# First loads of an MLP kernel on one queue, and the first transposes in two groups

## The chip, the cores and the metric

The kernel runs on one core of a Trainium2 chip. The metric is the device time of one execution in microseconds; 0.2% of it is about 0.8 us. A core has a matrix engine (TensorE, PE in the profile, with weight loads listed as PEld), VectorE (DVE), ScalarE (ACT), GpSimd (POOL) and SyncE (SP), which here only starts transfers. Each engine works through its own list of instructions in order, and engines wait for each other through semaphores. Transfers from memory are started by SP or ACT and carried out by 16 DMA engines.

## The reference

A layer norm without scale, a matrix product with bias, GELU, and a second product with bias. x is 2048 x 1024, w1 is 1024 x 3584, w2 is 3584 x 1024, all bf16.

```python
def _layernorm(x, axis=-1, eps=1e-5):
    m = jnp.mean(x, axis=axis, keepdims=True)
    v = jnp.var(x, axis=axis, keepdims=True)
    return (x - m) / jnp.sqrt(v + eps)

def reference(x, w1, b1, w2, b2):
    y = _layernorm(x, axis=-1)
    h = _gelu(jnp.einsum("bsd,df->bsf", y, w1) + b1)
    return jnp.einsum("bsf,fd->bsd", h, w2) + b2
```

## The kernel before

The 2048 rows of x are cut into 16 tiles of 128 and four blocks of four tiles. For each block the first product runs over 28 rows of output (`r`, 128 features each), each with 8 steps over the model dimension (`dt`, 128 each) and 512 columns (the rows of x in that block); GELU on ACT writes `hT_sb`. Then the second product makes eight output pieces of 128 x 512, each of 28 matmuls, and VectorE adds b2. Both products need their inputs with the contracted dimension on the partitions, so tiles of x are transposed.

Blocks 1 to 3 are normalised and transposed on VectorE under the matmuls of the block before. Block 0 has nothing to hide under, and its start is written out by hand; this is the part that the change touches.

**Raw tiles.** Tiles 0 to 2 (`N_RAW`) are transposed by PE before they are normalised. `pe_T` (L366) takes parts (tile, half) and a bank: the transposes of a half (four of 128 columns, `HALVES`) go to PSUM, ACT copies them to `yT_sb` (L386) and signals `te<tile>_<half>`. Matmuls run on the raw data, and the normalisation is put right afterwards: a column with a one beside the data (L259) gives each row's sum of weights, ACT copies it (`act_cs`, L526), and VectorE corrects each of the first seven PSUM banks with it and with rows that hold minus the mean and the reciprocal deviation (`ops_corr`, L535, the instructions of L537 and L540). GELU (L419) follows. `ops_fix` (L332) makes the centred `yT_sb` for the later rows of block 0.

**The first wave.** Seven rows (`R`) are held open in seven PSUM banks: rows 0 to 4 in `ps_1`, row 5 in the second bank of `ps_2`, row 6 in the first. The eighth bank, `t`, takes transposes, and the two of `ps_2` also serve for that before their rows start. `cells(rows, dts, t0, t1)` (L512) issues one matmul for each row and dt over the columns of tiles t0 to t1. It waits for the copies of those tiles and for the part of w1. Row 7 follows in bank t (`mm1_row`, L432), and row 8 reuses the bank of row 0, after row 0's GELU.

**Clock fillers.** `warm` (L484) issues matmuls on a constant, whose result is overwritten. 24 run at the start.

**Loads.** Each load is one transfer. `x0a` is the first half of tile 0's columns (128 KB); `xrb` the second halves of tiles 0 to 2 in one (384 KB); `w0` to `w7` are w1 for the first seven rows, one dt each (224 KB); `w8` and on are w1's later columns. SP issues `SP_FIRST_LOADS`, and then all others; ACT issues `x1a` and `x2a` (L227 to L230) ahead of its table load. SP spends about 0.47 us from one issue to the next.

**Order on the engines around the change.** PE: fillers, transposes of tile 0 and of tile 1 (first halves), cells of rows 0 to 4 with dt 0 and tile 0, transposes of tile 2, cells with tile 1, then both tiles together, then tile 2, then dt 2; then the second halves, which need `xrb`, and the rest of the wave; tile 3 last. VectorE (`head`, L492 to L507): statistics of the three first halves, of the three second halves, of tile 3, mean and deviation, transposes of these into rows, b1, the three fixes, the seven corrections. GpSimd spreads the rows over the partitions (L497).

Of the kernel before, what the change touches and what calls it, by code (L numbers as in the profile page):

```python
# [13 lines left out]
TPB = TB // P  # L14
R_WAVE = 7
NB1 = 5
NB2 = 2
NOB = 2
TAIL_PIECES = (384, 128)
WARM = 24  # L20
N_RAW = 3
RC = N_RAW * P
HALVES = (0, 4, 8)
W1_CHUNK_COLS = (512, 512, 1024, 640)
N_W2_CHUNKS = 4
SP_FIRST_LOADS = ("x0a", "w0", "w1", "w2", "xrb", "w3", "w4", "x3a", "x3b", "w5", "w6", "w7", "b1", "w8")
ACT_FIRST_LOADS = ("x1a", "x2a")

T_PE_START = 4.2
T_DVE_START = 26.0  # L30
# [54 lines left out]
def bass_standalone__mixer_channel_mlp__prompt_kernel(  # L85
# [13 lines left out]
    DT = D // P  # L99
# [6 lines left out]
    assert HC <= 512 and DT * P * 2 <= 2048 and FT >= 4 and FT <= P  # L106
    R = max(1, min(R_WAVE, FT - 2, NB1 + NB2))
    assert NB1 + NB2 + 1 <= 8 and NB2 == 2
    assert HALVES[-1] == DT and 0 < N_RAW < TPB

    w1_chunks = [(j, j + 1, 0, R * P) for j in range(DT)]
    c0 = R * P
# [24 lines left out]
    with ExitStack() as es:  # L137
# [32 lines left out]
        sp = _Prog(None)  # L170
        pe = _Prog("s_pe")
        act = _Prog("s_act")
# [3 lines left out]
        est = {}  # L176

        dma_bytes = [0.0]
        dma_q = [sp]
        x_ev = {}  # L180
        w1_issued = set()

        def dma(dst, src, sig, nbytes, waits=()):
            dma_q[0].op(lambda e, dst=dst, src=src: e.dma_start(dst, src), waits=waits, sig=sig, sem="d_" + sig, inc=16)
            dma_bytes[0] += nbytes
            est[sig] = DMA_T0 + dma_bytes[0] / DMA_BYTES_PER_US

        def load_x_tile(i):
            dma(x_sb[:, i, :], xf[i * P:(i + 1) * P, :], f"x{i}", P * D * 2)
            x_ev[i] = (f"x{i}", f"x{i}")  # L190
# [7 lines left out]
        def load_w1(ci):  # L198
            j0, j1, a, b = w1_chunks[ci]
            dma(w1_sb[:, j0:j1, a:b], w1v[:, j0:j1, a:b], f"w1c{ci}", (j1 - j0) * P * (b - a) * 2)  # L200
            w1_issued.add(ci)
# [5 lines left out]
        def issue(item):  # L207
            if item == "xrb":
                dma(x_sb[:, 0:N_RAW, HC:D], xf[0:N_RAW * P, HC:D].rearrange("(t p) d -> p t d", p=P), item,
                    N_RAW * P * HC * 2)  # L210
                for i in range(N_RAW):
                    x_ev[i] = (f"x{i}_0", item)
            elif item[0] == "x" and item[-1] in "ab":
                i, h = int(item[1:-1]), "ab".index(item[-1])
                dma(x_sb[:, i, h * HC:(h + 1) * HC], xf[i * P:(i + 1) * P, h * HC:(h + 1) * HC], f"x{i}_{h}",
                    P * HC * 2)
                x_ev[i] = (f"x{i}_0", f"x{i}_1")
            elif item == "b1":
                b1v = b1.rearrange("(t q a) -> q t a", q=4, a=32)
                for q in range(4):  # L220
                    dma(b1r_sb[32 * q:32 * q + FT, :], b1v[q], f"b1{q}", F // 2, waits=["b1z"])
            elif item[0] == "x":
                load_x_tile(int(item[1:]))
            elif item[0] == "w" and int(item[1:]) < len(w1_chunks):
                load_w1(int(item[1:]))

        dma_q[0] = act  # L227
        for item in ACT_FIRST_LOADS:
            issue(item)
        dma_q[0] = sp  # L230
        for item in SP_FIRST_LOADS:
            issue(item)
        for i in range(TPB):
# [16 lines left out]
        for b in range(2, NB):  # L250
# [5 lines left out]
                waits=["ones"], sig="ident")  # L256
# [11 lines left out]
        def op_stats(i, h):  # L268
            return (lambda e, i=i, h=h: e.bn_stats(st_sb[:, i, 6 * h:6 * (h + 1)], x_sb[:, i, h * HC:(h + 1) * HC]),  # L269
                    [x_ev[i][h]], f"st{i}_{h}", 0.65)  # L270

        def op_aggr(i):
            if i >= TPB:
                pool.op(lambda e, i=i: e.tensor_tensor(out=rstd_sb[:, i:i + 1], in0=mv_sb[:, i, 1:2],  # L274
                                                       in1=nhalf[:, i:i + 1], op=ALU.pow),
                        waits=[f"mv{i}", "nhalf"], sig=f"rstd{i}")
            return (lambda e, i=i: e.bn_aggr(mv_sb[:, i, :], st_sb[:, i, :]),  # L277
                    [f"st{i}_0", f"st{i}_1", "eps"], f"mv{i}", 0.33)
# [20 lines left out]
        y_ev = {}  # L299
# [32 lines left out]
        def ops_fix(i):  # L332
            s0, s1 = i * P, (i + 1) * P
            return [(lambda e: e.tensor_tensor(out=yT_sb[:, 0, :, s0:s1], in0=yT_sb[:, 1, :, s0:s1],  # L334
                                               in1=row_sb[:, 0:1, s0:s1].to_broadcast([P, DT, P]), op=ALU.add),
                     ["row0", f"te{i}_0", f"te{i}_1"], f"fx{i}v", 1.25)]

        yT_ev = {}
        mm1_done = {}
# [19 lines left out]
        def dve_put(o):  # L359
            dve.op(o[0], waits=o[1], sig=o[2])  # L360
# [4 lines left out]

        def pe_T(parts, bname):  # L366
            bap = t_bank[bname]
            nb = HALVES[1]
            last = f"tp{parts[-1][0]}_{parts[-1][1]}"
            w0 = ["ident"] + ([bank_read[bname]] if bname in bank_read else [])  # L370
            copies = []
            for n, (i, k) in enumerate(parts):
                j0, j1 = HALVES[k], HALVES[k + 1]
                buf, s0 = (1 if i < N_RAW else 0), i * P
                o = n * nb * P
                for j in range(j0, j1):
                    waits = (w0 if n == 0 else []) + [x_ev[i][k] if i < N_RAW else y_ev[i][j]] if j == j0 else []
                    pe.op(lambda e, i=i, j=j, o=o + (j - j0) * P: e.transpose(  # L378
                        out=bap[:, o:o + P], in_=x_sb[:, i, j * P:(j + 1) * P], identity=ident[:, :]),
                        waits=waits, sig=(f"tp{i}_{k}" if j == j1 - 1 else None))  # L380
                    yT_ev.setdefault(i, [None] * DT)[j] = f"te{i}_{k}"
                src = bap[:, o:o + (j1 - j0) * P].rearrange("p (j s) -> p j s", j=j1 - j0)
                copies.append((yT_sb[:, buf, j0:j1, s0:s0 + P], src, f"te{i}_{k}"))
                pe_t[0] += (j1 - j0) * 0.056
            for dst, src, sig in copies:
                act.op(lambda e, dst=dst, src=src: e.copy(out=dst, in_=src), waits=[last], sig=sig)  # L386
                bank_read[bname] = sig
# [96 lines left out]
        def warm(n, gate=None):  # L484
            for _ in range(n):
                pe.op(lambda e: e.matmul(ps_1[:, 0, 0:P], lhsT=unit, rhs=unit,  # L486
                                         start=True, stop=True), waits=[gate] if gate else [])

        act.op(lambda e: e.preload_act_table(ACT.Sqrt))
        warm(WARM)  # L490
        raw = list(range(N_RAW))
        head = [op_stats(i, h) for h in range(2) for i in raw] + [op_aggr(i) for i in raw]  # L492
# [3 lines left out]
        for k in range(2):  # L496
            pool.op(lambda e, k=k: e.partition_broadcast(  # L497
                row_sb[:, k, 0:RC], rvt_sb[0:1, k * N_RAW:(k + 1) * N_RAW, :].rearrange("p v s -> p (v s)")),
                waits=["rvt", "row1c", "scr"], sig=f"row{k}")
        pool.op(lambda e: e.tensor_tensor(out=scr_sb[:, 1, :], in0=scr_sb[:, 0, :], in1=nhalf[:, :], op=ALU.pow),  # L500
                waits=["row1"])
        h = DT // 2
        FX = [f"fx{i}v" for i in raw]
        for i in raw:
            head += ops_fix(i)
        for o in head:
            dve_put(o)  # L507

# [3 lines left out]
        def cells(rows, dts, t0, t1, by_row=False):  # L512
            n0, n1 = t0 * P, t1 * P + (1 if t1 == N_RAW else 0)
            order = [(r, dt) for r in rows for dt in dts] if by_row else [(r, dt) for dt in dts for r in rows]
            for r, dt in order:
                bank = wave[r][0]
                w = [yT_ev[i][dt] for i in range(t0, t1)] + (["rone"] if n1 > RC else [])
                if r not in started:
                    w += [bank_read[k] for k in (f"{bank[0]}_{bank[1]}",) if k in bank_read]
                pe_cell(r, dt, 1, n0, n1, bank, w, f"cw_{r}" if dt == DT - 1 and n1 > RC else None,  # L520
                        r not in started, False, shared=True)
                started.add(r)
# [26 lines left out]
        def late_cells(t, rows, dts):  # L549
            for r in rows:  # L550
# [6 lines left out]
                        act_gelu(r, 0, TPB, wave[r][0], f"sb_{r}", f"g_0_{r}")  # L557
                        hT_row[(0, r)] = f"g_0_{r}"

        first, most, every = range(NB1), [*range(NB1), R - 1], range(R)  # L560
        pe_T([(0, 0)], "t")
        pe_T([(1, 0)], "2_0")
        cells(first, (0,), 0, 1)
        pe_T([(2, 0)], "2_1")
        cells(first, (0,), 1, 2)
        cells((R - 1,), (0,), 0, 2)
        cells(most, (1,), 0, 2)
        cells((NB1,), (0, 1), 0, 2)
        cells(every, (0, 1), 2, 3)
        cells(every[:4], (2,), 0, 3)  # L570
        pe_T([(0, 1), (1, 1)], "t")
        cells(every[4:], (2,), 0, 3)
        cells(first, (3,), 0, 3)
        pe_T([(2, 1)], "t")
        cells(every[NB1:], (3,), 0, 3)
        act.op(lambda e: e.activation(out=std_sb[:, :], in_=mv_sb[:, 0:TPB, 1], func=ACT.Sqrt, bias=0.0, scale=1.0),
               waits=[f"mv{i}" for i in range(TPB)], sig="std")
# [52 lines left out]
        while ci < len(crit) or fi < len(fill):  # L630
# [5 lines left out]
            if take_crit:  # L636
                rdy, o, _ = crit[ci]
                ci += 1
            else:
                rdy, o, _ = fill[fi]  # L640
# [46 lines left out]
```

## Time and profile before

| What | us |
|---|---|
| Runs shown: median (lowest to highest of three) | 396.92 (396.49 to 397.13) |
| The profiled execution: its time, its span | 397.14, 395.9 |
| PE busy in the span | 393.0 |
| First filler on PE | 0.83 |
| First transposes of tile 0, start | 3.50 |
| First copy by ACT, start and length | 4.12, 0.585 |
| First cell, start | 4.76 |
| Second halves (`xrb`): issue on SP, statistics of them on VectorE | 2.64, 8.18 |
| Their transposes on PE, start | 8.63 |
| Last first-layer matmul of row 7, row 8's first | 20.71, 20.87 |

The landings of the first loads, from the trace (the last of 16 DMA engines): x0a 3.36, x1a 3.54, w0 4.60, x2a 4.77, w1 5.97, w2 6.54, `xrb` 8.16, w3 8.88, w4 9.48, x3a 9.82, x3b 10.19, w5 10.79, w6 11.39, w7 12.01, w8 16.49.

A line of a group gives the engine, the line of the kernel, the operation, its output and input tiles and shapes, and the count; in a timeline the first two numbers are the start and the length in us, and in brackets stands how long the engine was idle before and which event ended that. The chain of waits gives start, length, engine, tile, line and count. A matmul's recorded length includes its passage through the array, so successive ones overlap, and the distance of their starts tells the rate.

### The profile page before, as it was taken

The numbers are of one execution on the slowest core, as the hardware profiler recorded it, in microseconds if no ns is written. First come the engines' busy times: TensorE is split into PE (matmuls) and PEld (weight loads), VectorE is DVE, ScalarE is ACT, GpSimd is POOL, SyncE is SP. The second block draws the span as 40 slices with busy tenths as digits, with TensorE's granted clock in tenths as the row PEclk, the third lists the DMA queues.
The fourth block names the chain that finished last, engine by engine and source line by source line (L and its number), as shares of the span: only waits on it lengthen the run. The fifth ranks groups of instructions, "written<-read, shape, count | busy, mean of one in ns | idle before, by whom it ended". The sixth has DMA issues, their size and how long they took to land.

```text
span 395.9 us, 4579 instructions
## 1 busy us (share of the span) xinstructions
PE 393.0 (99%) x1964; PEld 186.6 (47%) x1964; DVE 160.1 (40%) x336; ACT 83.7 (21%) x125; POOL 11.9 (3%) x28
## 2 busy tenths in 40 slices
PE   8999999999999999999999999999999999999998
PEld 7744444444444444444444444444444444444445
DVE  4998889988999405987100000001100000001011
ACT  3374330000144342000023443100003334400000
POOL 0121100011000100000000000000000000000000
DMA  7999940000000000000000000000000000000000
GB/s 256 365 378 387 388 167 14 28 26 14 28 0 0 2 0 2 27 17 24 26 13 2 0 0 2 13 13 28 21 21 13 0 2 0 0 15 26 13 28 27
DMA packets 16747, 23.62 MB, mean 60 GB/s; under 512 B 1240, under 2 KB 10456, under 8 KB 16728
## 3 DMA queue, kind: packets, MB, share of 16 engines
q1 hardware_dynamic: 16440, 23.08, 16.6%
q8 instruction: 15, 0.25, 0.3%
q10 hardware_dynamic: 288, 0.26, 0.2%
q14 instruction: 4, 0.03, 0.0%
HBM read 19.14 MB, written 4.19 MB: 59 GB/s over the span
## 4 chain that ended last, share of the span: by engine, by line
PE 99%; ACT 0%; DVE 0%; issue 0%
PE ps L462 49%; PE ps L410 41%; PE ps_t L410 8%; PE ps L486 1%; PE ps_t L378 0%; ACT yT_sb L386 0%; PE ps L378 0%; DVE o_sb L473 0%
## 5 line engine op out<-in xcount | busy, mean ns | idle before, releaser
L462 PE MATMUL ps<-w_sb,hT_sb 128*128 128x512 bf16 (+2 forms) x924 | 194.1, 373 | 0.0
L410 PE MATMUL ps<-yT_sb,w_sb 128*128 128x512 bf16 (+4 forms) x832 | 167.1, 360 | 0.3 <-ACT yT_sb L386 0.3
L462 PEld LDWEIGHTS ps<-w_sb,hT_sb 128*128 128x128 bf16 x924 | 89.3, 98 | 104.5
L410 PEld LDWEIGHTS ps<-yT_sb,w_sb 128*128 128x128 bf16 x832 | 78.1, 98 | 84.8 <-ACT yT_sb L386 0.5
L419 ACT ACTIVATE hT_sb<-ps,b_sb 128x512 bf16<-128x512 f32 x94 | 64.2, 688 | 235.6 <-PE ps L410 217.2
L473 DVE TENSOR_TENSOR o_sb<-ps,b_sb 128x512 bf16<-128x512 f32 (+2 forms) x33 | 22.3, 676 | 198.5 <-PE ps L462 198.4
L354 DVE STREAM_TRANSPOSE yT_sb<-x_sb 32x256 bf16<-32x256 bf16 x192 | 83.7, 436 | 21.6 <-PE ps_t L410 18.6
L410 PE MATMUL ps_t<-yT_sb,w_sb 128*128 128x512 bf16 (+2 forms) x152 | 34.0, 368 | 0.0
L269 DVE BATCH_NORM_STATS2 st_sb<-x_sb 128x6 f32<-128x512 bf16 x32 | 21.1, 674 | 6.0 <-DMA x_sb<-in_x_dram 5.8
L410 PEld LDWEIGHTS ps_t<-yT_sb,w_sb 128*128 128x128 bf16 x152 | 14.5, 98 | 16.4
L419 ACT ACTIVATE hT_sb<-ps_t,b_sb 128x512 bf16<-128x512 f32 x18 | 12.4, 687 | 18.0 <-PE ps_t L410 14.6
L545 DVE TENSOR_TENSOR ps<-ps,row_sb 128x384 f32<-128x384 f32 x17 | 9.3, 564 | 3.1 <-PE ps L410 2.7
L274 POOL TENSOR_TENSOR rstd_sb<-mv_sb,nhalf 128x1 f32<-128x1 f32 x12 | 6.5, 542 | 99.6 <-DVE mv_sb L277 99.6
L294 DVE TENSOR_SCALAR x_sb<-x_sb,mv_sb,rstd_sb 128x1024 bf16<-128x1024 bf16 x13 | 7.0, 541 | 1.9 <-POOL rstd_sb L274 1.3
L386 ACT COPY yT_sb<-ps_t 128x512 bf16<-128x512 bf16 x6 | 3.3, 587 | 4.9 <-PE ps_t L378 4.9
L537 DVE SCALAR_TENSOR_TENSOR ps<-row_sb,cs_sb,ps 128x385 f32<-128x385 f32 x7 | 4.3, 615 | 0.0
L540 DVE TENSOR_TENSOR ps<-ps,row_sb 128x385 f32<-128x385 f32 x7 | 4.0, 568 | 0.2
L277 DVE BATCH_NORM_AGGREGATE mv_sb<-st_sb 128x2 f32<-128x15 f32 x16 | 3.3, 214 | 1.2
L334 DVE TENSOR_TENSOR yT_sb<-yT_sb,row_sb 128x1024 bf16<-128x1024 bf16 x3 | 3.7, 1293 | 0.0
L486 PE MATMUL ps<-const-bfloat16-1.0 128*128 128x128 bf16 x24 | 2.7, 312 | 0.8 <-PEq L672 0.8
L500 POOL TENSOR_TENSOR scr_sb<-scr_sb,nhalf 128x16 f32<-128x16 f32 x1 | 2.9, 2947 | 8.4 <-issue 8.4
L486 PEld LDWEIGHTS ps<-const-bfloat16-1.0 128*128 128x128 bf16 x24 | 2.5, 148 | 0.8 <-issue 0.8
(33 smaller groups left out, 18.7 us busy)
## 6 DMA issues: line engine op xcount, KB each, us to landing
w_sb<-in_w_dram SPq DMA_DIRECT2D x4, 1792.0 KB, 18.1
out_dram<-o_sb SPq DMA_DIRECT2D x31, 128.0 KB, 1.7
x_sb<-in_x_dram SPq DMA_DIRECT2D x3, 1024.0 KB, 14.0
w_sb<-in_w_dram SPq DMA_DIRECT2D x2, 1024.0 KB, 9.2
w_sb<-in_w_dram SPq DMA_DIRECT2D x1, 2048.0 KB, 15.2
w_sb<-in_w_dram SPq DMA_DIRECT2D x8, 224.0 KB, 5.7
w_sb<-in_w_dram SPq DMA_DIRECT2D x1, 1280.0 KB, 16.3
x_sb<-in_x_dram SPq DMA_DIRECT2D x3, 128.0 KB, 5.6
```

Of the source, the lines that this page charges most:

```text
L269: return (lambda e, i=i, h=h: e.bn_stats(st_sb[:, i, 6 * h:6 * (h + 1)], x_sb[:, i, h * HC:(h + 1) * HC]), [x_ev[i][h]], f"st{i}_{h}", 0.65)
L274: pool.op(lambda e, i=i: e.tensor_tensor(out=rstd_sb[:, i:i + 1], in0=mv_sb[:, i, 1:2], in1=nhalf[:, i:i + 1], op=ALU.pow), waits=[f"mv{i} ...
L294: return (lambda e, i=i, c0=c0, c1=c1: e.tensor_scalar(out=x_sb[:, i, c0:c1], in0=x_sb[:, i, c0:c1], scalar1=mv_sb[:, i, 0:1], scalar2=rst ...
L354: res.append((lambda e, src=src, dst=dst: e.transpose(out=dst, in_=src), waits, (f"tr{i}" if lastop else None), 0.47))
L410: pe.op(lambda e: e.matmul(unit_bank(bank)[:, n0:n1], lhsT=w1_sb[:, dt, r * P:(r + 1) * P], rhs=yT_sb[:, buf, dt, n0:n1], start=start, sto ...
L419: act.op(lambda e, r=r, n0=n0, n1=n1, bank=bank: e.activation(out=hT_sb[:, r, n0:n1], in_=unit_bank(bank)[:, n0:n1], func=ACT.Gelu_apprx_tanh,
L462: pe.op(lambda e, st=st, ft=ft, c0=c0, c1=c1, bank=bank: e.matmul(ps_2[:, bank, 0:c1 - c0], lhsT=hT_sb[:, ft, st * P:(st + 1) * P], rhs=w2 ...
L473: crit.append((est[sig], (lambda e, ob=ob, c0=c0, c1=c1, bank=bank: e.tensor_tensor(out=o_sb[:, ob, c0:c1], in0=ps_2[:, bank, 0:c1 - c0], ...
L486: pe.op(lambda e: e.matmul(ps_1[:, 0, 0:P], lhsT=unit, rhs=unit, start=True, stop=True), waits=[gate] if gate else [])
L537: return [(lambda e: e.scalar_tensor_tensor(out=ap, in0=row_sb[:, 0, :], scalar=cs_ap[r], in1=ap, op0=ALU.mult, op1=ALU.add), [f"m1_0_{r}" ...
L540: (lambda e: e.tensor_tensor(out=ap, in0=ap, in1=row_sb[:, 1, :], op=ALU.mult), [f"sa_{r}", "row1"], f"sb_{r}", 0.56)]
L545: crit.append((est[wait_ev], (lambda e: e.tensor_tensor(out=ap, in0=ap, in1=row_sb[:, 1, 0:RC], op=ALU.mult), [wait_ev, "row1"], f"sc_{r}" ...
```

## The change

- ACT issues no loads any more. SP issues all, in the order x0a, w0, x1a, w1, x2a, w2, `xrb`, and on as before.
- The first half of tile 0 is transposed in two groups of two 128-column pieces, into two banks, with a copy of 256 columns each (`PARTS` in place of `HALVES`). Cells wait for the group that holds their dt.
- Three of the 24 fillers move behind these transposes.
- The cells that follow are reordered: dt 0 and dt 1 of tile 0 on their own, and then both of tile 1 on their own, where before dt 1 took both tiles at once. Tile 2's transposes come before tile 1's cells, in bank t.
- The three fixes are put into VectorE's list at a later place of the text; nothing else is put there between.

```diff
-WARM = 24
+WARM = 21
+FILL = 3
-HALVES = (0, 4, 8)
+PARTS = ((0, 4), (4, 8), (0, 2), (2, 4))
-SP_FIRST_LOADS = ("x0a", "w0", "w1", "w2", "xrb", "w3", "w4", "x3a", "x3b", "w5", "w6", "w7", "b1", "w8")
-ACT_FIRST_LOADS = ("x1a", "x2a")
+SP_FIRST_LOADS = ("x0a", "w0", "x1a", "w1", "x2a", "w2", "xrb", "w3", "w4", "x3a", "x3b", "w5", "w6", "w7", "b1", "w8")
...
-        dma_q[0] = act
-        for item in ACT_FIRST_LOADS:
-            issue(item)
-        dma_q[0] = sp
         for item in SP_FIRST_LOADS:
             issue(item)
...
-                     ["row0", f"te{i}_0", f"te{i}_1"], f"fx{i}v", 1.25)]
+                     ["row0"] + list(dict.fromkeys(yT_ev[i])), f"fx{i}v", 1.25)]
...
-            nb = HALVES[1]
+            nb = DT // 2
-                j0, j1 = HALVES[k], HALVES[k + 1]
+                j0, j1 = PARTS[k]
-                    waits = (w0 if n == 0 else []) + [x_ev[i][k] if i < N_RAW else y_ev[i][j]] if j == j0 else []
+                    waits = (w0 if n == 0 else []) + [x_ev[i][j // nb] if i < N_RAW else y_ev[i][j]] if j == j0 else []
...
-        first, most, every = range(NB1), [*range(NB1), R - 1], range(R)
-        pe_T([(0, 0)], "t")
-        pe_T([(1, 0)], "2_0")
+        first, every = range(NB1), range(R)
+        pe_T([(0, 2)], "t")
+        pe_T([(0, 3)], "2_0")
+        warm(FILL)
         cells(first, (0,), 0, 1)
-        pe_T([(2, 0)], "2_1")
-        cells(first, (0,), 1, 2)
-        cells((R - 1,), (0,), 0, 2)
-        cells(most, (1,), 0, 2)
-        cells((NB1,), (0, 1), 0, 2)
+        pe_T([(1, 0)], "2_1")
+        cells(first, (1,), 0, 1)
+        pe_T([(2, 0)], "t")
+        cells(first, (0, 1), 1, 2)
+        cells((R - 1, NB1), (0, 1), 0, 2, True)
         cells(every, (0, 1), 2, 3)
```

More of the change, by code (lines that the diff above doesn't have):

```diff
@@ L108, in bass_standalone__mixer_channel_mlp__prompt_kernel @@
     assert NB1 + NB2 + 1 <= 8 and NB2 == 2
-    assert HALVES[-1] == DT and 0 < N_RAW < TPB
+    assert PARTS[1][1] == DT and 0 < N_RAW < TPB
     w1_chunks = [(j, j + 1, 0, R * P) for j in range(DT)]
@@ L178, in bass_standalone__mixer_channel_mlp__prompt_kernel @@
         dma_bytes = [0.0]
-        dma_q = [sp]
         x_ev = {}
@@ L183, in dma @@
         def dma(dst, src, sig, nbytes, waits=()):
-            dma_q[0].op(lambda e, dst=dst, src=src: e.dma_start(dst, src), waits=waits, sig=sig, sem="d_" + sig, inc=16)
+            sp.op(lambda e, dst=dst, src=src: e.dma_start(dst, src), waits=waits, sig=sig, sem="d_" + sig, inc=16)
             dma_bytes[0] += nbytes
@@ L503, in bass_standalone__mixer_channel_mlp__prompt_kernel @@
         FX = [f"fx{i}v" for i in raw]
-        for i in raw:
-            head += ops_fix(i)
         for o in head:
@@ L574, in bass_standalone__mixer_channel_mlp__prompt_kernel @@
         pe_T([(2, 1)], "t")
+        for i in raw:
+            for o in ops_fix(i):
+                dve_put(o)
         cells(every[NB1:], (3,), 0, 3)
```

## The prediction

> **What bounds the kernel now.** I read the page first (busy time, then the chain that ended last), then the chain in order of time for the first 22 us, then the timeline of each engine there, the waits, and the issues and landings of the first loads. On the page TensorE is the bound:
>
> ```profile
> span 395.9 us, 4579 instructions
> ...
> PE 393.0 (99%) x1964; PEld 186.6 (47%) x1964; DVE 160.1 (40%) x336; ACT 83.7 (21%) x125; POOL 11.9 (3%) x28
> ...
> PE 99%; ACT 0%; DVE 0%; issue 0%
> ```
>
> From 20.87 us to 394 us PE never pauses, so this change can move only the time at which PE reaches that dense part. The chain up to there (start, duration, what):
>
> ```profile
> 0.83 2.72 PE ps L486 x24
> 3.54 0.55 PE ps_t L378 x4
> 4.10 0.02 issue
> 4.12 0.59 ACT yT_sb L386
> 4.72 0.05 issue
> 4.76 0.72 PE ps L410 x5
> 5.48 0.43 PE ps L378 x4
> 5.91 2.89 PE ps L410 x32
> 8.79 0.45 PE ps_t L378 x8
> ```
>
> The reader is to see three things. The 24 fillers end just before the first transposes. PE then idles while ACT copies tile 0 (the only real gap). And the clock is low at first: four transposes take 0.43 us at 5.48, eight take 0.45 us at 8.79. In the timeline, 128-column matmuls start 107 ns apart until 6.12 us and 56 ns apart afterwards; I call 6.12 the switch.
>
> At the other end of the ramp stands a second bound, which the chain doesn't show because it ends in a tie. The timeline around 20.8 us:
>
> ```profile
> 20.22 0.81 PE L410 MATMUL ps_t<-yT_sb,w_sb 128*128 128x384 bf16 x4
> 20.83 0.14 PEld L410 LDWEIGHTS ps<-yT_sb,w_sb 128*128 128x128 bf16 x2 [0.18 <-ACT hT_sb L419]
> 20.87 0.38 PE L410 MATMUL ps<-yT_sb,w_sb 128*128 128x512 bf16 x1
> ```
>
> Row 8 of block 0 reuses the PSUM bank of row 0, so its weight load waits for row 0's GELU (20.09 to 20.78). PE's own arrival is 20.71 + 0.16 = 20.87: no time is lost, and none is spare. What feeds that GELU is VectorE, almost without a gap since one load:
>
> ```profile
> 3.39 2.10 DVE L269 BATCH_NORM_STATS2 st_sb<-x_sb 128x6 f32<-128x512 bf16 x3 [2.19 <-DMA x_sb<-in_x_dram]
> 8.18 1.88 DVE L269 BATCH_NORM_STATS2 st_sb<-x_sb 128x6 f32<-128x512 bf16 x3 [2.69 <-DMA x_sb<-in_x_dram]
> ...
> 15.19 3.73 DVE L334 TENSOR_TENSOR yT_sb<-yT_sb,row_sb 128x1024 bf16<-128x1024 bf16 x3
> 18.85 0.61 DVE L537 SCALAR_TENSOR_TENSOR ps<-row_sb,cs_sb,ps 128x385 f32<-128x385 f32 x1
> ```
>
> The second line waits for `xrb`, the second halves of tiles 0 to 2, issued at 2.64 and landing 5.5 us later:
>
> ```profile
> x_sb<-in_x_dram SPq DMA_DIRECT2D x1, 384.0 KB, 5.5
> ```
>
> So the dense part begins at the later of two times: PE's own arrival, and `xrb`'s landing (8.16) + 12.6 us of VectorE and ACT work + 0.1. Both are 20.87 today.
>
> **The change, part by part.**
>
> *x0a alone at the head.* Today x0a and x1a share the DMA engines and land at 3.36 and 3.54; the transposes start at 3.50. The stretch from 2 to 3 us moved 287 GB/s, that from 3.4 to 5.0 moved 359. No row shows x0a alone. Bounds: nothing saved, or all of x1a's 131 KB taken out from ahead of its end, 131/355 = 0.37 us. Since the two interleaved nearly packet for packet I take 0.37: transposes at T = 3.13.
>
> *Three fillers fewer at the start.* 3 x 107 ns = 0.32; the last leaves its slot at 3.02 instead of 3.34. PE waits for x0a there anyway, so this is worth nothing; if x0a is not earlier, PE idles 0.48 instead of 0.16.
>
> *Tile 0 in two groups.* Before: four transposes, copy of 512 columns, first cell 1.26 after T (3.50 to 4.76). After: two transposes end at T + 0.37, ACT starts 0.04 later, copies 256 columns. ACT copies took 0.585 for 512 columns and 0.165 for 5, so 256 cost 0.375; 0.055 to PE: first cell at T + 0.84 = 3.97. That is 0.42 less. The extra copy costs ACT about 0.16 us of fixed time; ACT was idle from 5.20 to 5.94 and from 6.53 to 9.28, which hides it.
>
> *Three fillers behind the transposes*: T + 0.43 to T + 0.75, before the copy is done at T + 0.78, so hidden; with the clock up they take 0.17, hidden still.
>
> *Cells reordered.* Five 256-column cells become ten of 128: 2 x 57 - 109 = 5 ns each, 0.02 us in all.
>
> *Banks.* Tile 2 now goes through bank t, whose copy of tile 0 is long read; the `xrb` transposes then wait for tile 2's copy, done by about 6.8, against 8.5. Row 5 and 6's cells wait for copies done by 6. Nothing.
>
> *The fixes' place in the text.* VectorE's order is the same; the first fix waits for three copies instead of two, all over by 10.4, against 15.19. Nothing.
>
> *Two issues off ACT's queue* (0.89 us): the table load can start at 0.8 instead of 1.70 and end at 2.1. First copy after 3.5, so nothing.
>
> *Two issues more on SP.* SP spends 0.47 us per issue, so everything behind x2a is issued up to 0.95 later: w2 (0.95), `xrb` (2.64 to 3.58), w3, w4, x3a, x3b, w5 to w7, the four parts of b1, w8. No load waits for another's data; what counts is whether the issue becomes later than the turn of its data. x0a's first packet came 1.02 after its issue; `xrb`'s came at 5.08, which is 2.44 after. So 1.42 is spare against 0.95, and the bytes ahead of `xrb` are the same 1.08 MB. Its landing stays at 8.16; the bounds are -0.4 (fifteen of its engines had landed by 8.03, ten by 7.44) and +0.95. w8 turns tight (issue about 9.55 + 1.02 = 10.57, its data's turn 10.27), 0.3 late at most, and it landed at 16.49 for a use at 19.1. x3a and x3b have 0.4 and 0.6 us on VectorE, w5 to w7 more than 1 us on PE, b1 1.7.
>
> The Trainium skill, "DMA: Bandwidth & Descriptors", section "Issuing engines are not separate DMA queues", says that transfers started by several engines share the same 16 DMA engines and that issuing from several saves only the sequencer's issue time. That speaks against this change: it would give 0.95 us of issue time back to SP for nothing in bandwidth. If that time stood on the path the sum would be 397.9; by the 1.42 us of spare lead it is hidden, and the forecast stands.
>
> *The other landings.* By the bytes ahead, interpolated between today's landings (0.32 MB at 3.54, 0.62 MB at 4.77, 0.85 MB at 5.20 on fifteen engines and 5.97 on the last): w0 at 3.7 (today 4.60), x1a 4.2, w1 5.0, x2a 5.2 to 6.0 (today 4.77), w2 as today.
>
> *PE's new order in time, low clock to 6.12.* Cells of tile 0, dt 0, 3.97 to 4.51; tile 1's transposes to 4.93; dt 1 waits for w1, 5.0 to 5.55; tile 2's transposes to 5.97; then ten cells of tile 1, two at 107 and eight at 57, to 6.6; 4 x 109, 14 x 57, 4 x 163 to 8.49. Today the `xrb` transposes start at 8.63: a lead of about 0.14, or a lag of 0.15 where x2a lands at 6.0. The 0.8 us won at the first cell has shrunk because 0.32 of it is fillers, the rest ran at half the clock, and the switch stays where it is.
>
> **Sum.** Lead at 8.5: 0.14. At 20.87 the GELU of row 0 hasn't moved, so what is kept is what the weight load had spare, 0.04 at most. The profiled run of 397.14 (span 395.9 and 1.24 around it) would become 397.10. The shown runs have a median of 396.92, 0.22 less; to that I apply the same 0.04 and round: **396.9**, no change that can be told. Own range, from the bounds of `xrb` short of a late issue and of x2a: 396.5 to 397.4.
>
> **Rivals.**
>
> *The later issue reaches `xrb`.* Slower. Place: SP's queue; it decides once the lead of issue over first packet falls under 0.95. Price: VectorE's whole line shifts, row 8's weight load with it, up to 0.95: 397.9. For it: `xrb` is the one load with a waiter (2.69 us of VectorE idle), and SP's issues are back to back. Against: the 1.42 spare.
>
> *The clock switch slips.* Slower. If the low clock lifts only after a stretch that is busy enough, PE's new gaps may spoil the stretch that ended at 6.12. Between the first filler (0.83) and the switch PE idled 0.16 + 0.46 = 0.62 us and the clock still lifted; the new order has 3.02 to 3.13, 3.88 to 3.97 and the waits for w1 and x2a: 0.2 to 0.9. It would decide from some point over 0.62, so only where x2a is at its latest. How long the next try lasts no row shows: at least the 1.36 since the last gap (4.76 to 6.12), at most the whole 5.29; the middle is 3.3. At half rate that costs 0.7 to 2.6, middle 1.65: 398.5. The Trainium skill, "TensorE: Matmul & The Clock Gate", Part 1, has the gate look at a free-running window of about 3.4 us, which an estimate by that page would price at 1.7. The trace's single switch doesn't contradict it, and no row shows the window itself.
>
> *Both lines move up.* Faster. If `xrb`'s last engines come with the others (7.44), VectorE gains 0.7 and PE could start its transposes there only if it were that early; its lead is 0.14, and at most 0.38 with an earlier switch. So 396.5, within the same class; a gain over 0.8 us needs a cause that I don't see in the rows.
>
> *It doesn't do what it says* (x0a no earlier): T = 3.50, first cells at 4.34, lead near 0: 396.9 again.
>
> **How the numbers follow.** 0.2% of 396.9 is 0.8 us, about what a measurement of this kernel can tell from no change: below 396.13 is faster, above 397.71 slower. Forecast, with the last rival and the small gain: 0.66. Late `xrb`: 0.13. Switch slipped: 0.10. Something faster by more than 0.8, most likely a switch and landings that both come early: 0.11. Slower is 0.13 + 0.10 less the part of a late `xrb` that stays under 0.8 us, counted as 0.02: 0.21; same 0.68. The range takes in the late `xrb`, the small gains and about half of the slips: 396.1 to 398.4.
>
> **What would show it.** Right: transposes at about 3.1, first cells at about 4.0, `xrb`'s issue near 3.6 but VectorE's second statistics still at about 8.2, and PE's weight load at 20.8 waiting for the GELU of row 0, longer than 0.18. Wrong: VectorE's second statistics at 9 (late issue); 107 ns between matmuls beyond 6.5 (slip); or a GELU of row 0 that ends before 20.2, with PE there too.

## The result, and the profile after

The changed kernel takes 398.59 us (median of six, 397.93 to 399.62) against 396.91 (396.49 to 397.13): a ratio of 1.0047, interval 1.0029 to 1.0065. That is slower by 1.7 us, and the six spread over 1.7 us where those of before spread over 0.6. The profiled execution is the slowest of the six: 399.62, span 398.4. Its parts are read here against the profiled execution of before, 397.14.

The chain of waits of the changed kernel in its first 24 us (start, duration, what) begins with SP's issues up to 2.64 and then a transfer, where PE's fillers stood before:

```profile
2.64 4.04 DMA x_sb<-in_x_dram
6.68 0.05 issue
6.72 0.61 PE ps_t L373 x4
7.33 3.92 PE ps L405 x32
11.25 0.45 PE ps_t L373 x8
...
21.74 1.75 PE ps_t L405 x16
23.49 0.05 issue
23.54 0.59 PE ps L405 x2
```

The transfer is x2a, issued at 2.64 and landed at 6.68. The second halves' transposes, which stood at 8.79 in the chain, stand at 11.25. From there to row 8 each piece takes as long as before, so 2.5 us of the loss lie ahead of 11.25; row 8 starts at 23.33 (20.87 before; the first of its matmuls has no record, its weight loads start at 23.17 and 23.33). The start of row 8 is the whole account: in all thirteen executions traced for this document the time less that start is 376.27 to 376.30 us. The timeline of the engines shows the beginning as forecast:

```profile
3.09 0.37 PE L373 MATMUL ps_t<-ident,x_sb 128*128 128x128 bf16 x2
3.50 0.37 ACT L381 COPY yT_sb<-ps_t 128x256 bf16<-128x256 bf16 x1 [1.43 <-PE ps_t L373]
4.02 0.69 PE L405 MATMUL ps<-yT_sb,w_sb 128*128 128x128 bf16 x5
5.91 0.45 PEld L405 LDWEIGHTS ps<-yT_sb,w_sb 128*128 128x128 bf16 x5 [1.04 <-DMA w_sb<-in_w_dram]
6.72 0.34 PEld L373 LDWEIGHTS ps_t<-ident,x_sb 128*128 128x128 bf16 x4 [0.36 <-DMA x_sb<-in_x_dram]
```

The first cell comes at 4.02 instead of 4.76. But the cells of dt 1 wait 1.04 us for w1, and tile 2's transposes 0.36 for x2a. Then PE is busy, but slowly: the next 128-column matmuls start 107 ns apart until 10.3 us (6.1 before), and the piece of 32 cells takes 3.92 us where a like piece, of 640 columns more, took 2.89.

VectorE's second line moved as well. In its timeline:

```profile
8.98 1.88 DVE L264 BATCH_NORM_STATS2 st_sb<-x_sb 128x6 f32<-128x512 bf16 x3 [1.59 <-DMA x_sb<-in_x_dram]
...
14.02 0.18 DVE L279 RECIPROCAL rv_sb<-std_sb 128x3 f32<-128x3 f32 x1 [1.38 <-ACT std_sb L573]
```

`xrb` arrives 0.8 later (8.96 against 8.16), and VectorE then waits 1.38 for ACT's square root, which stands behind the copies of PE's late transposes in ACT's list (0.33 before). Row 0's GELU starts at 21.94 and ends at 22.63. Row 8 starts 0.7 later still, so in this execution PE, and not VectorE, sets the end of the ramp.

Why did the loads come late, with the same bytes in nearly the same order? The engines' busy time by stretch has the transfers in its last two columns (share of the DMA engines' time, GB/s); before the change, then after:

```profile
1.80:5.20 3.40, 3.15 (x30) 2.69 (x28) 1.70 (x3) 2.26 (x3) 0.07 (x2) 1.00 0.91 301
5.20:9.00 3.80, 3.80 (x46) 3.44 (x45) 1.11 (x3) 0.58 (x1) 0.00 (x0) 1.00 0.96 304
```

```profile
1.80:5.20 3.40, 3.32 (x30) 2.71 (x27) 1.39 (x2) 0.94 (x4) 0.07 (x2) 1.00 0.82 223
5.20:9.00 3.80, 2.99 (x23) 2.52 (x24) 0.71 (x2) 1.15 (x2) 0.29 (x1) 1.00 0.92 301
```

In the first 3.4 us of the stream one queue moved 223 GB/s, two moved 301; afterwards they are level. By 5 us packets of 705 KB had started instead of 960. Cut more finely, the same view is level up to 3.5 us too (244 GB/s against 248), and the whole difference arises between 3.5 and 5.0 (193 against 359). The time of issue isn't what holds the transfers back there: x0a's first packet came 1.02 us after its issue, and by 4.5 us 635 KB had started, while loads of 1081 KB (x0a to w2) had been issued by 3.11.

### The profile page after: what moved, and what is told of

Same layout as the page of the kernel before. It is cut to its first block, busy times and chain, and to the rows that moved or that the text cites. A ratio compares the mean times of both kernels' runs of the same rounds, so it can differ in the third digit from the quotient of the medians.

```text
span 398.4 us, 4557 instructions
## 1 busy us (share of the span) xinstructions
PE 393.0 (99%) x1935; PEld 188.0 (47%) x1969; DVE 160.3 (40%) x336; ACT 83.9 (21%) x126; POOL 11.9 (3%) x28
## 4 chain that ended last, share of the span: by engine, by line
PE 97%; DMA 1%; issue 1%; SPq 0%; DVE 0%
PE ps L457 48%; PE ps L405 41%; PE ps_t L405 8%; DMA x_sb<-in_x_dram 1%; PE ps_t L373 0%; SPq L183 0%; DVE o_sb L468 0%
## 5 line engine op out<-in xcount | busy, mean ns | idle before, releaser
L405 PEld LDWEIGHTS ps<-yT_sb,w_sb 128*128 128x128 bf16 x837 | 79.5, 100 | 85.7 <-DMA w_sb<-in_w_dram 1.0
L381 ACT COPY yT_sb<-ps_t 128x512 bf16<-128x512 bf16 (+1 forms) x7 | 3.7, 557 | 7.8 <-PE ps_t L373 7.8
```

The costliest lines, as they stand in the source:

```text
L405: pe.op(lambda e: e.matmul(unit_bank(bank)[:, n0:n1], lhsT=w1_sb[:, dt, r * P:(r + 1) * P], rhs=yT_sb[:, buf, dt, n0:n1], start=start, sto ...
```

## The experiments

Three causes were to be told apart: the single queue (late loads), PE's idle time (late clock), and the new order of groups and cells. The bytes of the packets started by 5 us and the landings of w1 and `xrb` are from each trace, as is the time of the last matmul at the low rate (107 ns for 128 columns). "Full clock from" is the trace's own record of the granted clock, where it holds one. The ratio and its interval are taken over all timed executions and need not equal the ratio of the two medians.

| Kernel | KB by 5 us | w1, `xrb` | low rate until | full clock from | median (range), us | ratio to before, interval |
|---|---|---|---|---|---|---|
| before (its first profile) | 960 | 5.97, 8.16 | 6.1 | no record | 396.91 (396.49 to 397.13) | |
| changed (its first profile) | 705 | 5.87, 8.96 | 10.3 | 10.27 | 398.59 (397.93 to 399.62) | 1.0047, 1.0029 to 1.0065 |
| changed, again | 678 | 6.03, 8.60 | 9.5 | 9.65 | 399.22 (397.96 to 399.60) | 1.0048, 1.0034 to 1.0061 |
| changed, two queues | 963 | 5.29, 8.03 | 8.3 | 8.45 | 398.47 (397.17 to 399.47) | 1.0034, 1.0021 to 1.0047 |
| before, one queue | 638 | 6.40, 8.52 | 9.8 | 9.90 | 399.76 (397.86 to 401.29) | 1.0057, 1.0034 to 1.0079 |
| changed, waits filled | 740 | 5.97, 9.09 | 5.7 | no record | 398.21 (398.07 to 398.48) | 1.0030, 1.0018 to 1.0042 |
| changed, two queues, filled | 990 | 5.32, 8.23 | 4.4 | 4.90 | 397.49 (396.92 to 398.08) | 1.0011, 1.0002 to 1.0019 |
| changed, w0 to w2 on ACT, filled | 897 | 5.28, 7.45 | 3.3 | 4.06 | 397.48 (397.23 to 398.76) | 1.0014, 1.0005 to 1.0023 |
| before, filled | 942 | 6.04, 8.29 | 4.6 | 4.73 | 397.17 (396.67 to 397.51) | 1.0002, 0.9993 to 1.0010 |
| before, one queue, x first | 779 | 6.15, 9.21 | 9.5 | 9.55 | 397.83 (397.56 to 399.39) | 1.0031, 1.0019 to 1.0043 |
| before, w2 on ACT, filled | 856 | 6.38, 7.54 | 4.5 | 4.64 | 397.34 (396.88 to 398.00) | 1.0001, 0.9993 to 1.0010 |
| before, w2 on ACT | 951 | 6.48, 8.12 | 4.1 | 4.50 | 397.42 (396.89 to 399.98) | 1.0012, 0.9998 to 1.0025 |
| before, 16 fillers | 951 | 5.56, 8.04 | 8.9 | 9.09 | 398.48 (397.74 to 398.70) | 1.0028, 1.0017 to 1.0038 |

The kernel before had medians of 397.0 to 397.25 beside these. The traced execution is one of those timed (but for the first profile of the kernel before, 397.14), so a rate or switch belongs to that one execution.

**When the clock lifts, from the records.** Eleven of the thirteen traces record the granted clock, and the record agrees with the distances of the matmuls' starts. (The PEclk column of the views above reads 1.00 where no record stands, and so also before the lift.) The recorded full clock lasts 389.12 us in six executions and 392.53 us in five: 114 and 115 times 3.413 us. So in these executions the clock was granted or not in steps of 3.41 us, and the steps lie differently against the kernel's start in each. PE's idle time in each step can be counted from the starts (107 ns busy for every 128 columns). All eleven steps at whose end the full clock came held 0.79 us of idle time or less. Every step before them held 0.86 or more: in the changed kernel 0.86 up to 3.44 us and 1.51 up to 6.86, with two queues 0.95 up to 5.03, with 16 fillers 1.49 up to 5.67. No run was made to test this reading.

**The changed kernel again**, unedited, on the chip of the next three.

> The changed kernel itself, on the chip of the three others. Main theory (one queue delivers the first loads later, PE idles for w1 and x2a, and the idle time delays the clock): 397.9 to 399.6, with w1 landing at about 5.9 and x2a at about 6.7, and a switch of the clock at 9 to 10.5 us. Rival (a disturbance of the one profile): loads and switch as before the change, time under 397.7.

Measured: 678 KB by 5 us, w1 at 6.03, x2a at 6.37, low rate until 9.5. The late loads and the late clock are there again, so neither was a disturbance of one profile. The twelve executions of the two runs lie in two groups, five at 397.93 to 398.09 and seven at 399.09 to 399.62, and both traced ones belong to the upper group.

**The queue alone, in both directions.** First the changed kernel with ACT issuing again:

```diff
-SP_FIRST_LOADS = ("x0a", "w0", "x1a", "w1", "x2a", "w2", "xrb", "w3", "w4", "x3a", "x3b", "w5", "w6", "w7", "b1", "w8")
+SP_FIRST_LOADS = ("x0a", "w0", "w1", "w2", "xrb", "w3", "w4", "x3a", "x3b", "w5", "w6", "w7", "b1", "w8")
+ACT_FIRST_LOADS = ("x1a", "x2a")
```

> The changed kernel with x1a and x2a back on ACT's queue; groups, fillers and order of the cells stay changed. Main theory (the single queue delivers late): w1 lands by 6.0, x2a by 4.8, xrb by 8.2 again, PE idles once (for w1, about 0.7), 396.7 to 397.4. Rival (the order of the cells, which asks for w1 before anything else of tile 1, does the harm): 398 or more, with idle time before dt 1 and a late switch.

Half a hit. Every load is back (963 KB, `xrb` 8.03), and PE doesn't wait for w1, which came early. But the median is 398.47, and neither theory gave the reason: x0a lands at 3.34 again, so 21 fillers leave 0.45 us of idle time ahead of the transposes and 0.5 ahead of the first cell (w0 at 4.54), and the low rate lasts to 8.3. In this execution the clock was late without late loads. Then the kernel before with one queue:

```diff
-SP_FIRST_LOADS = ("x0a", "w0", "w1", "w2", "xrb", "w3", "w4", "x3a", "x3b", "w5", "w6", "w7", "b1", "w8")
-ACT_FIRST_LOADS = ("x1a", "x2a")
+SP_FIRST_LOADS = ("x0a", "w0", "x1a", "w1", "x2a", "w2", "xrb", "w3", "w4", "x3a", "x3b", "w5", "w6", "w7", "b1", "w8")
+ACT_FIRST_LOADS = ()
```

> The kernel before with the loads on SP's queue alone, in the changed order; everything on PE stays as before. Main theory: the loads are late as in the changed kernel (xrb at about 9.0 instead of 8.2), VectorE's line shifts by 0.8, 397.7 or more; more still if PE's waits delay the clock. Rival (order of the cells): 396.9 within 0.3, since PE's old order needs w1 only at 6.3.

638 KB by 5 us, 1.0057: the queue alone costs as much as the whole change, in PE's old order. `xrb` came 0.4 rather than 0.8 late in the traced execution, and PE idled 1.6 us ahead of tile 2's transposes, for x2a, which landed at 6.75 (4.77 before).

**One queue, another order of loads**, in the kernel before:

```diff
-SP_FIRST_LOADS = ("x0a", "w0", "w1", "w2", "xrb", "w3", "w4", "x3a", "x3b", "w5", "w6", "w7", "b1", "w8")
-ACT_FIRST_LOADS = ("x1a", "x2a")
+SP_FIRST_LOADS = ("x0a", "x1a", "x2a", "w0", "w1", "w2", "xrb", "w3", "w4", "x3a", "x3b", "w5", "w6", "w7", "b1", "w8")
+ACT_FIRST_LOADS = ()
```

> The kernel before with all loads on SP's queue, but the three x tiles first and then w0, w1, w2, so large and small transfers don't alternate. If one queue alone delivers slower whatever the order: under 780 KB by 5 us, xrb at 8.5 or later, 397.7 or more. Rival (the alternation of x and w1 is what slows the stream): 900 KB or more by 5 us and xrb at 8.2.

779 KB, only just under the 780 of the first expectation, `xrb` at 9.21, 1.0031. That is more than the other four traces with one queue (638 to 740) and far from 900, so the alternation of x and w1 is at most part of the cause. Five traces with one queue lie at 638 to 779 KB, eight with two at 856 to 990. They part between 3.5 and 5.0 us, at 147 to 255 GB/s against 302 to 380; from 1.8 to 3.5 they do not differ (233 to 248 against 223 to 256).

**The clock alone.** In the changed kernel the two waits were filled with matmuls on the constant, into bank t:

```diff
+        hold(10, "te0_2")
         cells(first, (1,), 0, 1)
+        hold(4, "te0_2")
         pe_T([(2, 0)], "t")
```

> The changed kernel with ten more fillers before the cells of dt 1 and four before the transposes of tile 2, where PE idled 1.08 and 0.41 us. They write to bank t, which is free then. If idle time on PE delays the clock: the switch comes by 7.5 us although the loads are as late as in the changed kernel, and the time falls to about 397.7, which the 0.8 us later xrb sets through VectorE. If the clock doesn't depend on these gaps: 398 to 399.6 as the changed kernel, with the switch at 9 to 10.5.

The loads are as late as ever (740 KB, `xrb` 9.09), but the low rate ends at 5.7, the median falls by 1.0 us against the changed kernel beside it (398.21 to 399.22), and the range shrinks from 1.6 to 0.4. Of the changed kernel's six executions four lie at 399.2 to 399.6 and two at 398.0, below all five of the filled one: the fillers took away the late executions and did not speed up the others. With so few runs the size is loose (by the two ratios 0.7 us, with intervals that overlap). What is left stands where the prediction put VectorE's line. The timeline of this kernel:

```profile
20.95 0.26 PEld L405 LDWEIGHTS ps_t<-yT_sb,w_sb 128*128 128x128 bf16 x2
21.02 0.69 ACT L414 ACTIVATE hT_sb<-ps,b_sb 128x512 bf16<-128x512 f32 x1 [4.04 <-DVE ps L538]
21.54 0.57 DVE L538 TENSOR_TENSOR ps<-ps,row_sb 128x385 f32<-128x385 f32 x1
21.76 0.33 PEld L405 LDWEIGHTS ps<-yT_sb,w_sb 128*128 128x128 bf16 x3 [0.55 <-ACT hT_sb L414]
21.99 0.38 PE L405 MATMUL ps<-yT_sb,w_sb 128*128 128x512 bf16 x1 [0.39 <-ACT hT_sb L414]
```

Now the weight load waits 0.55 us for row 0's GELU, and PE idles with it. (The first matmul of row 8 has no record here, since two weight loads start at 21.76 and 21.78; it starts at 21.78, and PE idles about 0.34.) The tie of before, 20.87, has opened by 0.9, and `xrb` is 0.9 later.

The same cause without late loads, in the kernel before:

```diff
-WARM = 24
+WARM = 16
```

> The kernel before with 16 fillers at the start instead of 24, so that PE idles about 1.0 us before the first transposes instead of 0.16; loads, groups and order as before the change. If idle time on PE delays the clock by itself: the loads land as before the change (xrb at about 8.2, 940 KB or more by 5 us), but the switch comes later than 6.1 in some executions, the spread grows to 1 us or more and the median rises by 0.3 to 1.5. If only late loads matter: 397.0 within 0.3 and a spread under 1.

The loads are as before (951 KB, `xrb` 8.04), PE idles 1.0 us ahead of the transposes, and the median rises by 1.2 us, to 398.48. The spread is 0.96, not above 1: nearly every execution is late. In its chain of waits:

```profile
4.78 0.69 PE ps L410 x5
5.47 0.43 PE ps L378 x4
5.89 4.32 PE ps L410 x32
10.21 0.45 PE ps_t L378 x8
```

The cells of tile 0 start at 4.78, as early as in the kernel before (4.76). The 32 cells behind them take 4.32 us instead of 2.89, because the low rate lasts to 8.9. That is the price of the clock in this execution, 1.4 us, with nothing changed but the idle time ahead of the transposes.

**Both causes taken away** from the changed kernel: two queues, and its gaps filled.

```diff
-WARM = 21
-FILL = 3
+WARM = 25
+FILL = 7
...
+        hold(3, "te0_2")
         cells(first, (1,), 0, 1)
```

> The changed kernel with x1a and x2a back on ACT's queue, and the gaps that PE had there filled: 25 fillers at the start, 7 behind tile 0's transposes, 3 before the cells of dt 1. Theory (two separate causes: the queue makes the loads late and so VectorE's line, the gaps make the clock late): with both taken away the time is 396.5 to 397.1 and the runs lie within 0.6 of each other, the switch by 6.2. Rival (the new order of the cells costs time by itself): 397.5 or more.

397.49, a ratio of 1.0011 (to 1.0019), in the traced execution row 8 at 20.90. This lies just between the two expectations and spreads over 1.2 us rather than 0.6. Of the 0.47% some 0.1% remains with the new order of groups and cells and these fillers; what it is, the one trace doesn't tell.

**The other side of the tie.** The kernel before with its gaps filled (25 fillers at the start, 4 behind tile 1's transposes):

```diff
-WARM = 24
+WARM = 25
+FILL = 4
...
         pe_T([(1, 0)], "2_0")
+        warm(FILL)
```

> The kernel before with its two gaps on PE filled: 25 fillers at the start instead of 24, and 4 behind tile 1's transposes. Nothing else. Theory (the gaps decide when the clock lifts, and VectorE's line sets the floor): the spread of the runs shrinks and the median falls by 0 to 0.4, 396.5 to 397.0. Rival (the fillers stand in the way of the copy and the cells): 397.2 or more.

The low rate ends at 4.6, 1.5 us earlier, and nothing comes of it: 397.17, 1.0002, which lies between the two expectations. The timeline at row 8:

```profile
20.00 0.81 PE L411 MATMUL ps_t<-yT_sb,w_sb 128*128 128x384 bf16 x4
20.22 0.69 ACT L420 ACTIVATE hT_sb<-ps,b_sb 128x512 bf16<-128x512 f32 x1 [4.03 <-DVE ps L541]
20.96 0.11 PEld L411 LDWEIGHTS ps<-yT_sb,w_sb 128*128 128x128 bf16 x2 [0.53 <-ACT hT_sb L420]
```

The weight load waits 0.53 for the GELU instead of 0.18. A gain on PE alone is lost here, as the prediction had it.

**Moving both lines up.** w2 on ACT's queue brings `xrb` forward by one place; with and without the fillers of the last experiment.

```diff
-SP_FIRST_LOADS = ("x0a", "w0", "w1", "w2", "xrb", "w3", "w4", "x3a", "x3b", "w5", "w6", "w7", "b1", "w8")
-ACT_FIRST_LOADS = ("x1a", "x2a")
+SP_FIRST_LOADS = ("x0a", "w0", "w1", "xrb", "w3", "w4", "x3a", "x3b", "w5", "w6", "w7", "b1", "w8")
+ACT_FIRST_LOADS = ("x1a", "x2a", "w2")
```

> The kernel before with w2 moved from SP's queue to ACT's, behind x2a, so that xrb comes up one place earlier on SP's and shares with w2; and with PE's two gaps filled as in the run before it (25 and 4). Theory (row 8 starts at the later of PE's arrival and VectorE's line, and both were level): with both moved up, xrb lands at 7.5 to 7.8, row 0's GELU starts at 19.5 to 19.8, row 8 at 20.5 to 20.7, and the time is 0.2 to 0.4 under the kernel before: 396.6 to 396.9 against its 397.0. Rival (the delivery of xrb isn't what sets VectorE's line, or w1 and w2 get late instead): 397.0 or more.

> The same move of w2 without the fillers: VectorE's line alone is earlier. Theory: PE's own arrival (20.87 with a switch at 6.1) is then what counts, so 397.0 within 0.2, and a spread of the runs that goes with the switch. Rival: 396.7 or less, if VectorE's line was the only bound.

A miss. VectorE's line moved as hoped in the filled one (`xrb` 7.54, GELU at 19.62), but w1 now shares with w2 and lands at 6.38, PE idles 0.65 us for it, and row 8 starts at 21.0: no gain (1.0001). Without fillers `xrb` hardly moved (8.12) and the median is 397.42 (1.0012, the interval just reaching 1), one execution at 399.98. The last try put w0, w1 and w2 on ACT's queue in the changed kernel, with 25, 4 and 2 fillers:

```diff
+SP_FIRST_LOADS = ("x0a", "x1a", "x2a", "xrb", "w3", "w4", "x3a", "x3b", "w5", "w6", "w7", "b1", "w8")
+ACT_FIRST_LOADS = ("w0", "w1", "w2")
```

> The changed kernel with w0, w1 and w2 on ACT's queue and all else on SP's, 25 fillers at the start, 4 behind tile 0's transposes, 2 before dt 1. If it is the number of queues that counts for delivery, the bytes moved by 5 us are 900 KB or more, as with the old split, and xrb lands earlier than 8.0 because it shares with the weights instead of standing behind them; the time 396.3 to 397.0. If only the old split delivers: 700 to 800 KB by 5 us, 397.7 or more.

Delivery is good with this split too (897 KB, just under the 900 expected), and `xrb` comes at 7.45. But x0a shares with w0 and lands at 4.03 instead of 2.95, so PE's first transposes start 0.7 us later than in the kernel before, and row 8 starts at 20.94. The median is 397.48. None of the kernels tried beats the kernel before.

## Why the prediction was wrong

- **What bounds the kernel** held: a tie at row 8 between PE's arrival and a line that begins with `xrb`'s landing. Filling the gaps of the kernel before gained nothing; holding the clock up in the changed kernel left row 8 behind `xrb`, both 0.9 later. In every trace the time went with the start of row 8.
- **The head of the list** held in each step: x0a at 2.95 (0.4 earlier), transposes at 3.09 (3.13 forecast), ACT's copy of 256 columns 0.37 (0.375), first cell at 4.02 (3.97), fillers hidden.
- **The step that failed is "The other landings"**, with "Its landing stays at 8.16" beside it. Both took the rate of delivery from two queues and applied it to one: so many bytes ahead, so late a landing. The stream's first 3.4 us moved 223 GB/s instead of 301, all of the difference after 3.5 us. So w0 and x1a still came nearly as forecast (3.88 against 3.7, 4.22 against 4.2), but w1 came at 5.87 against 5.0, x2a at 6.68 against 5.2 to 6.0, w2 at 7.61 against 6.54, `xrb` at 8.96 against 8.16. The bound of +0.95 held `xrb` for the wrong reason. The late issue was in fact hidden: `xrb` was issued at 3.58, and its first packet came at 5.95, still 2.4 after.
- **The rule of the Trainium skill** weighed there ("DMA: Bandwidth & Descriptors", "Issuing engines are not separate DMA queues": a second issuer saves only issue time) gave the right warning with the wrong mechanism. In these traces the second queue added delivery, 856 to 990 KB by 5 us against 638 to 779, in a stretch where issue time was not the limit.
- **The rival "The clock switch slips"** is half of what happened. The point from which it decides was put above 0.62 us of idle time; the changed kernel had 1.6 us before 6.8, and the records, read as above, put the point between 0.79 and 0.86 us within one step. The next try was taken to last 3.3 us, the middle of its bounds; the step is 3.41. The price was taken as 1.65; the medians give 1.2 for fewer fillers before the change, and between the two groups of the changed kernel's executions lie 1.3 to 1.4. Its chance of 0.10 was too low because the waits for w1 and x2a were sized by the failed step.
- **The rival of a late `xrb`** is the other half, its price 1.2 us with the clock held up (398.21 against 397.0), where at most 0.95 was priced. The changed kernel run beside them lost 2.2 (399.22); what is over 1.2 is the clock's part only by subtraction. The two are one event: the loads' lateness makes the idle time.
- **"Wrong" signs** were named rightly: VectorE's second statistics at 9, and 107 ns beyond 6.5, were both there. But the first stood there as the sign of a late issue, and the issue was not the cause.

Why one queue delivers less is only partly seen. In the traces some packets, nearly all of them 1792-byte packets of w1, take 200 to 900 ns instead of 74: between 2 and 5.2 us, 25 in the changed kernel and 11 before. Perhaps another queue lets an engine go on with other loads when one queue's packet is stuck. The Trainium skill, "DMA: Bandwidth & Descriptors", "Queues, rings and completion order", has each DMA engine take packets in turn from the queues that have work. The trace agrees as far as it goes: x0a on SP's queue and x1a on ACT's moved side by side from 2.25 to 2.93 us before the change. And with w2 on ACT's queue slow packets were nearly as many (21 and 24) and yet 951 and 856 KB came. Against it as the whole reason: between 3.5 and 5.0 us the DMA engines' busy share was 0.83 in the changed kernel, so part of the time they stood idle with issued loads waiting. None of this was tested, nor why those packets are slow. Also open: why the changed kernel's executions fall into two groups. Steps of the clock that lie differently in each execution would do it, since a step that ends before PE's wait for w1 brings the full clock one step sooner, but none of the lower group was traced.

## What to carry to other kernels

A rate of delivery read off a trace belongs to the number of queues that were active: before moving the first loads to one queue, compare GB/s in stretches with one and with two. Where the matrix engine starts on a low clock, count a wait in the ramp twice, once as idle time and once for what it can do to the clock, and bridge it with fillers. Before making one line of a ramp earlier, look whether another meets it; here both must move, and moving one was worth nothing.

## What the runs showed of the hardware

- One microsecond without matmuls ahead of the first transposes, with everything else alike, kept the low rate (107 ns for 128 columns) until 8.9 us instead of 6.1 and cost 1.2 us at the median.
- The record of the granted clock moves in steps of 3.41 us whose place differs between executions. In the eleven traces that hold it the full clock came at the first step with 0.79 us or less of idle time on PE, and never at one with 0.86 or more. With 25 fillers at the start it came at 4.06 to 4.90 us, 3.2 to 4.1 after the first filler.
- One queue and two delivered alike until 3.5 us and parted between 3.5 and 5.0 us, at 147 to 255 GB/s (five traces) against 302 to 380 (eight).
